# A recurrence with decay and a token mixer on one core: scores in half chunks, and the rest through a copied product of keys and values

## The chip, the cores and the metric

The kernel runs on one core of a Trainium2 chip. The metric is the device time of one execution in microseconds (us). A core has the engines PE (matrix multiply, with PEld its weight load), DVE, ACT and POOL for work on vectors, and SP, which here issues transfers. SBUF is the working memory of 128 partitions, PSUM the memory that PE writes, in eight banks of 512 float32 columns a partition.

## The reference

Four batches, eight heads, 768 tokens, 48 values a head. For each batch and head a 48 by 48 state is carried over the tokens; the mixer behind it works on the eight heads side by side (384 columns).

```python
for t in range(S):
    cur = einsum('bhd,bhe->bhde', u[None] * k[t], v[t])
    y[t] = einsum('bhd,bhde->bhe', r[t], state + cur)
    state = w[t][..., None] * state + einsum('bhd,bhe->bhde', k[t], v[t])
x = y, heads side by side                      # 4 x 768 x 384
W_tok = (x @ w_q) @ (x @ w_k)^T / 8            # taken token by token with x
out = relu(W_tok-mix of x) @ w_out
```

The mixer's two weights are 384 by 64, so its mix is computed as (x w_q) times ((x w_k)^T x), and then relu and w_out.

## The kernel before, in words

The tokens of a batch are cut into three units of 256 tokens, twelve units in all (`unit`, L438). A unit holds two chunks c of 128 tokens. Heads go in pairs: head 2hp in partitions 0 to 63, head 2hp+1 in 64 to 127, 48 of 64 used. With decays as logarithms, the running product inside a chunk becomes a matmul with a triangular matrix, and everything in a chunk can be computed at once.

The steps of a unit, by the names in the code: loads of wg, kg, rg and vg, each 384 KB, on SP (`load`, L301; in batch 3 v comes as `vw` for the whole batch, L306). ACT takes the logarithm lw (L462), POOL casts k and r to bf16 (L472) and v (L581). PE sums the logarithms into PSUM (cw, with CM); ACT takes exp both ways: ep (L500) and en (L505). PE transposes k and r (kr); ks is the copied transpose of k (ACT or DVE), qT = r times k for the bonus (L536), RT = r times ep (L550), KT = k times en (L557 on DVE, L560 mostly on POOL). PE reorders v from two tokens a partition into chunks (vp), and the copy is VB. The bonus is qT times UB (dps), copied as dd, times VB on POOL: Vd (L618).

For each chunk, A is KT by RT: 128 by 128 scores for each of eight heads, 16 matmuls a unit. DVE multiplies them by the mask US into AM (L638, 128x1024 from PSUM, 24 times). KT is also transposed (kb) and scaled into kd, and sn = kd by VB plus the older state gives the next state SB (L696). The result y is yi = RT by the older SB, plus ya = AM by VB (16 matmuls a unit), scaled and added to Vd as X (L754). X is transposed (xt, XT), multiplied by the mixer weights (wk, wq, copied as QK); at the end of a batch T = QK by X (copied as TS), then mx, relu (MX), fp with w_out, os (L393, L399) and the store (L878).

PE has several tile shapes: the full array, two halves by rows (48 or 64 partitions of input), halves by columns, and quarters of 64 by 64. Every matmul has line L250 (`mm`).

The order on each engine is written out: each step has a number in RANK, and ALT says which engine takes a step where there is a choice (D is DVE, A is ACT, P is POOL, E and e are PE, e in parts of the array). `Plan.order` (L86) walks the queues with a duration for each step and gives PSUM banks (one, `bank`, or two, `wide`) and buffers from rings; RINGS has two of most buffers. WARM adds up to 30 multiplies by zeros (Z), where ALT says E.

Of the kernel before, what the change touches and what calls it, by code (L numbers as in the profile page):

```python
# [10 lines left out]
F32 = mybir.dt.float32  # L11
# [22 lines left out]
class Plan:  # L34
# [51 lines left out]
    def order(self):  # L86
# [85 lines left out]
    3, 0, 0, 0, 5, 18, 0, 0, 21, 1, 2, 0, 0, 0, 1, 0, 0, 2, 0, 0, 3, 0, 0, 1, 3, 4, 4, 4, 2, 5,  # L172
    3, 5, 11, 3, 6, 4, 1, 5, 2, 5, 17, 8, 24, 9, 9, 10, 25, 10, 18, 7, 10, 6, 12, 7, 20, 8, 27,
    11, 30, 37, 33, 31, 15, 73, 31, 82, 32, 6, 0, 0, 4, 0, 0, 7, 0, 0, 8, 0, 0, 9, 6, 7, 26, 11,
    12, 23, 28, 10, 13, 12, 14, 8, 34, 14, 36, 15, 15, 40, 17, 45, 21, 41, 18, 48, 20, 53, 23,
    57, 64, 59, 58, 27, 74, 29, 87, 35, 9, 0, 0, 10, 0, 0, 11, 0, 0, 12, 0, 0, 13, 11, 12, 38,
    16, 17, 39, 42, 16, 18, 19, 14, 13, 47, 20, 49, 22, 18, 55, 24, 60, 25, 56, 22, 61, 26, 68,
    69, 72, 70, 30, 80, 36, 88, 36, 94, 38, 97, 40, 109, 49, 47, 0, 0, 102, 42, 120, 53, 50, 0,
    0, 134, 58, 141, 62, 51, 0, 0, 13, 0, 0, 14, 0, 0, 15, 0, 0, 17, 0, 0, 19, 16, 17, 50, 23,
    21, 63, 66, 25, 28, 29, 20, 19, 71, 28, 77, 33, 23, 75, 32, 79, 34, 76, 30, 81, 35, 85, 37,  # L180
    86, 91, 89, 90, 40, 100, 41, 104, 44, 16, 0, 0, 20, 0, 0, 22, 0, 0, 23, 0, 0, 24, 22, 25,
    67, 26, 27, 84, 93, 38, 42, 41, 39, 26, 95, 39, 110, 47, 32, 98, 47, 106, 49, 92, 37, 101,
    46, 105, 48, 115, 119, 118, 117, 54, 128, 59, 139, 60, 19, 0, 0, 21, 0, 0, 24, 0, 0, 25, 0,
    0, 31, 24, 27, 83, 34, 33, 96, 99, 43, 44, 45, 29, 28, 103, 43, 111, 48, 33, 113, 52, 108,
    50, 107, 45, 112, 51, 122, 124, 126, 125, 57, 138, 61, 156, 68, 164, 73, 167, 76, 185, 82,
    54, 0, 0, 176, 78, 211, 97, 52, 0, 0, 183, 81, 213, 99, 53, 0, 0, 26, 0, 0, 28, 0, 0, 27, 0,
    0, 31, 0, 0, 46, 31, 30, 116, 52, 51, 114, 121, 53, 56, 55, 34, 35, 129, 56, 136, 62, 40,
    131, 60, 140, 65, 127, 58, 135, 61, 143, 68, 149, 151, 153, 154, 73, 165, 75, 188, 86, 29,
    0, 0, 30, 0, 0, 33, 0, 0, 32, 0, 0, 50, 36, 38, 123, 55, 54, 132, 137, 57, 64, 63, 39, 37,
    142, 66, 159, 69, 47, 163, 76, 160, 75, 144, 67, 148, 70, 157, 74, 170, 172, 174, 175, 82,  # L190
    187, 83, 199, 91, 35, 0, 0, 37, 0, 0, 34, 0, 0, 38, 0, 0, 59, 41, 42, 145, 65, 64, 146, 150,
    69, 71, 72, 44, 43, 155, 67, 158, 70, 49, 177, 83, 166, 77, 161, 71, 168, 78, 179, 181, 184,
    182, 86, 191, 89, 205, 94, 212, 98, 223, 103, 237, 109, 55, 0, 0, 231, 105, 245, 111, 56, 0,
    0, 234, 109, 248, 113, 57, 0, 0, 36, 0, 0, 41, 0, 0, 40, 0, 0, 45, 0, 0, 46, 0, 0, 63, 46,
    45, 162, 72, 74, 169, 171, 79, 81, 80, 51, 53, 189, 84, 56, 195, 91, 186, 87, 190, 88, 194,
    90, 198, 92, 200, 203, 201, 204, 95, 210, 96, 221, 102, 39, 0, 0, 44, 0, 0, 42, 0, 0, 66,
    50, 48, 173, 77, 79, 178, 180, 80, 85, 84, 52, 54, 192, 87, 59, 207, 98, 197, 93, 193, 88,
    202, 94, 206, 96, 214, 217, 219, 216, 104, 226, 104, 233, 110, 43, 0, 0, 48, 0, 0, 49, 0, 0,
    85, 55, 57, 196, 92, 89, 93, 90, 208, 209, 95, 102, 99, 97, 100, 101, 58, 220, 101, 60, 61,
    215, 103, 224, 106, 218, 100, 222, 105, 225, 229, 227, 230, 228, 232, 107, 235, 106, 238,  # L200
    239, 112, 111, 108, 236, 107, 240, 241, 108, 113, 242, 244, 243, 110, 246, 114, 115, 250,
    253, 118, 116, 59, 0, 0, 61, 0, 0, 247, 112, 116, 251, 252, 114, 119, 58, 0, 0, 60, 0, 0,
    249, 117, 115, 254, 255, 117, 118, 119, 62, 0, 0, 6, 147, 19, 35, 13, 51, 65, 43, 44, 29,
    16, 2, 46, 78, 0, 21, 152, 52, 1, 62, 130, 32, 15, 8, 14, 54, 22, 9, 133, 7,
]
ALT = ("PPDEADAAEDAPPADEAAEAEAAPPDPEADAeDAAAAAAAAPPAPeADEAEAAPPDDEAAeAEDAPPDPeAAAEAAAAAAAAAPPDPE"
       "ADEDEAAPPAPeDAEDEAAPPDPeAAAEDAAAAAADAPPDPAeDEAAPPAPAEAeADPPAAAEADDEAADADDDAADADDAAAEeEEE"
       "eEEEEEeeEeeeEeeeeEeeEeeeE")
# [5 lines left out]
def kernel(  # L214
# [27 lines left out]
    WHOLE = (3,)  # L242
    DIRECT = (0, N - 1)

# [13 lines left out]
    def const(shape, dtype, name):  # L258
# [3 lines left out]
    EW = 132  # L262
# [3 lines left out]

    RINGS = dict(
# [4 lines left out]
        dd=(2, 2 * H, F32), Vd=(2, 2 * DM, BF16), AM0=(2, 1024, BF16), AM1=(2, 1024, BF16),  # L272
# [6 lines left out]
    used = dict.fromkeys(RINGS, 0)  # L279

    uT = const([C, NP * 2], F32, "uT")
    UB = const([C, NP * 2], BF16, "UB")
    wq_f = const([C, NK * DH], F32, "wqf")
    wk_f = const([C, NK * DH], F32, "wkf")
    wo_f = const([C, NK * DM], F32, "wof")
# [152 lines left out]
    def unit(n, batch):  # L438
# [53 lines left out]
        cws = add(("cw", n), {"E": 435}, f_cw, [ln], cw, [lw], mode=1)  # L492

        en, ep = ring("en"), ring("ep")
        ens, eps = {}, {}
        for cs in fine:
            w_ = 512 * len(cs)

# [438 lines left out]
```

## Time and profile before

| what | value |
| --- | --- |
| median of 3 runs | 105.81 us (105.46 to 107.37) |
| the profiled execution's own time | 104.84 us |
| its span, first to last instruction | 103.0 us |
| mean granted PE clock | 0.973 |
| PE, DVE, ACT, POOL busy | 89.3, 81.9, 80.5, 69.5 us |
| matmuls | 1898 |
| moved by DMA | 24.67 MB |
| last load (rg of unit 11) issued | 71.9 us |

A row of the page's fifth part reads: line, engine, operation, out<-in by tile names, sizes of out and in, count; then busy us and mean ns of one; then the idle time of the engine just before, and what ended it. A line of a stretch gives its length, then for PE, PEld, DVE, ACT and POOL the busy us and the count, then the granted clock, the busy share of DMA and GB/s. A line of the timeline gives the start, the length of the run from its first start to its last end, and the count.

### The profile page before, as it was taken

How to read it: one execution, taken by the hardware profiler on the slowest of the kernel's cores; microseconds unless marked ns; L12 is line 12 of the kernel's file. 1: busy time of each engine (PE TensorE's matmuls, PEld its weight loads, DVE VectorE, ACT ScalarE, POOL GpSimd, SP SyncE). 2: the span in 40 equal slices, each digit the busy share in tenths (PEclk: the TensorE clock that was granted, in tenths of full speed). 3: DMA queues.
4: the chain of work that ended last, by engine and by line, in shares of the span. 5: the costliest groups of instructions: out<-in, count | busy, mean ns of one | idle time of the engine just before them, and what ended most of it. 6: DMA issues, size and time to landing. Idle time of an engine off the chain costs nothing.

```text
span 103.0 us, 4462 instructions
## 1 busy us (share of the span) xinstructions
PE 89.3 (87%) x1898; PEld 64.3 (62%) x1898; DVE 81.9 (80%) x140; ACT 80.5 (78%) x121; POOL 69.5 (67%) x81
## 2 busy tenths in 40 slices
PE   5969994999799998999989899879899979999930
PEld 2234753567676966686785787756888648766610
DVE  6628995959989888998999998897999599882800
ACT  6376969769699997999999999888898766766650
POOL 6666393899899976789989997997978504100000
PEclk9999999669999999999999999999999999999995
DMA  1999999999999998999999996999992036204694
GB/s 29 296 325 325 328 259 253 311 296 269 324 255 260 311 293 221 293 282 276 315 314 308 244 293 175 225 166 213 279 376 76 6 153 235 77 0 159 262 353 152
DMA packets 56804, 24.67 MB, mean 240 GB/s; under 512 B 54480, under 2 KB 55632, under 8 KB 56784
## 3 DMA queue, kind: packets, MB, share of 16 engines
q1 hardware_dynamic: 56224, 24.19, 85.0%
q8 instruction: 15, 0.25, 0.9%
q10 hardware_dynamic: 560, 0.20, 0.7%
q14 instruction: 5, 0.04, 0.1%
HBM read 19.66 MB, written 4.72 MB: 237 GB/s over the span
## 4 chain that ended last, share of the span: by engine, by line
PE 51%; DVE 14%; ACT 10%; SPq 9%; DMA 6%; issue 4%; POOL 1%; DVEq 0%; POOLq 0%; ACTq 0%
PE PS L250 51%; SPq L302 9%; DMA kg<-in_k_dram 6%; DVE AM L638 5%; ACT ks L393 3%; DVE X L754 2%; DVE ks L399 2%; ACT ep L500 2%; DVE qT L536 2%; ACT os L393 1%; DVE RT L550 1%; ACT kd L395 1%; ACT en L505 1%; POOL k L472 1%; ACT lw L462 1%
## 5 line engine op out<-in xcount | busy, mean ns | idle before, releaser
L638 DVE TENSOR_TENSOR AM<-PS,US 128x1024 bf16<-128x1024 f32 x24 | 28.9, 1218 | 0.9 <-PE PS L250 0.6
L618 POOL TENSOR_TENSOR Vd<-VB,dd 128x768 bf16<-128x768 bf16 (+1 forms) x14 | 18.0, 1293 | 5.1 <-ACT dd L393 5.1
L560 POOL TENSOR_TENSOR KT<-ks,en 128x1024 bf16<-128x1024 bf16 x8 | 17.0, 2127 | 1.3 <-ACT ks L393 1.3
L500 ACT ACTIVATE ep<-PS 128x1024 bf16<-128x1024 f32 (+1 forms) x14 | 12.6, 918 | 1.7 <-PE PS L250 1.7
L250 PE MATMUL PS<-wo,MX 128*128 128x384 bf16 x72 | 13.4, 326 | 0.7 <-DVE AM L638 0.7
L505 ACT ACTIVATE en<-PS 128x1024 bf16<-128x1024 f32 (+1 forms) x14 | 12.4, 901 | 1.6 <-PE PS L250 1.2
L754 DVE SCALAR_TENSOR_TENSOR X<-PS,gx,Vd 128x768 bf16<-128x768 f32 (+1 forms) x13 | 12.4, 950 | 1.5 <-PE PS L250 1.4
L462 ACT ACTIVATE lw<-wg 128x768 bf16<-128x768 f32 x12 | 10.2, 848 | 4.1 <-DMA wg<-in_w_dram 4.1
L250 PEld LDWEIGHTS <-KT 48*128 48x128 bf16 (+1 forms) x312 | 10.0, 95 | 5.2 <-issue 3.5
L472 POOL CAST k<-kg 128x768 bf16<-128x768 f32 x12 | 9.9, 825 | 4.3 <-DMA kg<-in_k_dram 4.3
L393 ACT COPY os<-PS 128x768 f32<-128x768 f32 (+1 forms) x13 | 9.1, 704 | 3.4 <-PE PS L250 3.2
L472 POOL CAST r<-rg 128x768 bf16<-128x768 f32 x12 | 9.9, 826 | 2.5 <-DMA rg<-in_r_dram 2.4
L250 PE MATMUL PS<-RT,KT 48*128 48x128 bf16 x192 | 9.7, 221 | 0.9 <-DVE qT L536 0.7
L250 PE MATMUL PS<-Z 128*128 128x512 bf16 x23 | 9.2, 502 | 1.2 <-DVE uT L319 1.2
L250 PEld LDWEIGHTS <-MX 128*128 128x128 bf16 x72 | 6.5, 97 | 4.9 <-issue 1.1
L581 POOL CAST v<-vg 128x768 bf16<-128x768 f32 x9 | 7.9, 878 | 2.4 <-DMA vg<-in_v_dram 2.4
L550 DVE TENSOR_TENSOR RT<-PS,ep 128x1024 bf16<-128x1024 bf16 (+1 forms) x14 | 8.3, 607 | 1.0 <-ACT ks L393 0.5
L536 DVE TENSOR_TENSOR qT<-PS,ks 128x1024 bf16<-128x1024 bf16 x12 | 8.2, 682 | 0.9 <-PE PS L250 0.7
L395 ACT ACTIVATE kd<-PS,gk 128x384 bf16<-128x384 bf16 (+1 forms) x10 | 7.0, 712 | 1.7 <-PE PS L250 1.5
L696 DVE TENSOR_TENSOR SB<-PS,ep 128x192 bf16<-128x192 f32 x20 | 7.0, 349 | 1.7 <-PE PS L250 1.5
L250 PE MATMUL PS<-SB,RT 48*128 48x48 bf16 x160 | 7.1, 182 | 1.3
L405 ACT ACTIVATE MX<-PS 128x768 bf16<-128x768 f32 (+1 forms) x10 | 7.5, 753 | 0.7 <-PE PS L250 0.6
(83 smaller groups left out, 188.7 us busy)
## 6 DMA issues: line engine op xcount, KB each, us to landing
wg<-in_w_dram SPq DMA_DIRECT2D x12, 384.0 KB, 5.7
kg<-in_k_dram SPq DMA_DIRECT2D x12, 384.0 KB, 5.9
rg<-in_r_dram SPq DMA_DIRECT2D x12, 384.0 KB, 5.4
vg<-in_v_dram SPq DMA_DIRECT2D x9, 384.0 KB, 5.0
out_dram<-os SPq DMA_DIRECT2D x9, 384.0 KB, 3.1
vw<-in_v_dram SPq DMA_DIRECT2D x4, 288.0 KB, 6.1
out_dram<-os SPq DMA_DIRECT2D x5, 192.0 KB, 2.1
wof<-in_moe_w_out_dram SPq DMA_DIRECT2D x1, 576.0 KB, 5.6
```

The costliest lines, as they stand in the source:

```text
L250: return nc.tensor.matmul(o, l, rr, start=start, stop=stop, skip_group_check=True, is_transpose=trans)
L393: nc.scalar.copy(o, i)
L462: nc.scalar.activation(view(lw.tile, 0, [[64, H], [512, 2], [1, D]]), view(g["wg"].tile, 0, [[D2, H], [D, 2], [1, D]]), ACT.Ln, bias=0.0, ...
L472: op(view(o.tile, 0, [[64, H], [512, 2], [1, D]]), view(g[src].tile, 0, [[D2, H], [D, 2], [1, D]]))
L500: nc.scalar.activation(view(ep.tile, cs[0] * NP * EW + 66, [[EW, NP * len(cs)], [-65, 2], [1, 64]]), at(cw)[:, ds(cs[0] * 512, w_)], ACT.E ...
L505: nc.scalar.activation(en.tile[:, ds(cs[0] * 512, w_)], at(cw)[:, ds(cs[0] * 512, w_)], ACT.Exp, bias=0.0, scale=-1.0)
L536: lambda e: nc.vector.tensor_tensor(view(qT.tile, 0, [[512, 2], [1, 512]]), turned(512), view(ks.tile, 0, [[512, 2], [1, 512]]), ALU.mult),
L550: nc.vector.tensor_tensor(o, x, y, ALU.mult)
L560: x.tensor_tensor(o, view(ks.tile, cs[0] * 512, dims), y, ALU.mult)
L618: nc.gpsimd.tensor_tensor(Vd.tile[:, cols], VB.tile[:, cols], view(dd.tile, cs[0] * H, [[1, len(cs) * H], [0, D]]), ALU.mult)
L638: AMs[c] = add(("AM", n, c), {"D": 1221}, lambda e, c=c, A=A: nc.vector.tensor_tensor(view(AM[c].tile, 0, [[C, 8], [1, C]]), view(at(A), 0 ...
L754: nc.vector.scalar_tensor_tensor(view(X.tile, (2 * i + c0) * DM, [[DM, nc_], [1, DM]]), view(at(y), 0, [[512, nc_], [1, DM]]), gx, view(Vd ...
```

## The change

Scores are computed only within half chunks of 64 tokens. A is now a matmul of 64 by 64 for each head, chunk and half, on quarters of the array; the two halves of a chunk stand in the two halves of the partitions, so that one AM of 128x1024 holds a whole unit, where there were two (in the first and the last unit, two of 128x512). What the second half takes from the first goes through a product: kv = kd by VB over the first 64 tokens, 16 matmuls a unit, copied to the new tile KV (ACT or DVE) and scaled back. ya is now AM by VB on quarters, in two turns with a drain between, with KV by RT for the second half after each turn: 48 matmuls a unit instead of 16.

For this the tokens inside a chunk are ordered by halves of 64, and inside those even and odd tokens in 32s; masks, permutations and views follow. ep has a column more for each half (EW 136 instead of 132, steps of 34 and 68), which a new step sh copies, on POOL in nine units and on DVE in three; RT waits for sh. In units 0 and 1 (FULL) the transposes of k and r use the whole array: 8 matmuls of 128 columns instead of 16 on halves. vp always uses halves. In the last unit of a batch kb and kd are made for both chunks. `load_whole` issues four transfers where there were two. The bonus u is loaded in rows of heads (UR), cast, transposed by one multiply and copied as UB. RANK and ALT are new, and with them which engine takes which copy.

```diff
+        dd=(2, 2 * H, F32), Vd=(2, 2 * DM, BF16), AM=(2, 1024, BF16), KV=(2, NCHP * D, BF16),
...
+            def f_sh(e, cs=cs):
+                n4 = NP * len(cs)
+                op = nc.vector if e == "D" else nc.gpsimd
+                op.tensor_copy(view(ep.tile, cs[0] * NP * EW + 68, [[EW, n4], [1, 1]]),
+                               view(ep.tile, cs[0] * NP * EW + 32, [[EW, n4], [1, 1]]))
...
+                        if full:
+                            mm(view(o, place + hp * pair + j * 32,
+                                    [[NP * pair, 2], [64, 2], [1, 32]]), x, ID16, trans=True)
...
-                        mm(x[:, ds(hh * 512 + hp * C, C)],
-                           KT.tile[ds(hh * 64, D), ds((c * NP + hp) * C, C)],
-                           RT.tile[ds(hh * 64, D), ds((c * NP + hp) * C, C)])
+                        for q in range(2):
+                            cols = ds((c * NP + hp) * C + q * 64, 64)
+                            mm(x[ds(q * 64, 64), ds(hh * 512 + (c * NP + hp) * 64, 64)],
+                               KT.tile[ds(hh * 64, D), cols], RT.tile[ds(hh * 64, D), cols])
...
+        for cs in fine:
+            def f_AM(e, cs=cs):
+                dims = [[512, 2], [64, NP * len(cs)], [1, 64]]
+                nc.vector.tensor_tensor(
+                    view(AM.tile, cs[0] * NP * 64, dims), view(at(A), cs[0] * NP * 64, dims),
+                    view(US, 0, [[0, 2], [0, NP * len(cs)], [1, 64]]), ALU.mult)
...
+            def f_kv(e, cs=cs):
+                x = at(kv)
+                for c in cs:
+                    for h in range(H):
+                        hp, hh = divmod(h, 2)
+                        mm(x[ds(hh * 64, 64), ds((c * NP + hp) * D, D)],
+                           kd.tile[ds(0, 64), ds(64 + (c * H + h) * 128, 64)],
+                           VB.tile[ds(0, 64), ds(c * DM + h * D, D)])
...
+            def f_KV(e, cs=cs):
+                w_ = ds(cs[0] * NP * D, NP * D * len(cs))
+                copy(e, KV.tile[:, w_], at(kv)[:, w_], 1 / UNIT)
...
+        def local(turn, cs, begun):
+            for hp in range(NP):
+                for h in (2 * hp, 2 * hp + 1):
+                    for c in cs:
+                        q = c ^ turn
+                        o = of(c, h)[ds(q * 64, 64), :]
+                        mm(o, AM.tile[ds(q * 64, 64),
+                                      ds((h % 2) * 512 + (c * NP + hp) * 64, 64)],
+                           VB.tile[ds(q * 64, 64), ds(c * DM + h * D, D)],
+                           start=(not begun[c] and h == 0), stop=False)
+            for hp in range(NP):
+                for c in cs:
+                    hh = c ^ turn
+                    o = of(c, 2 * hp + hh)[ds(64, 64), :]
+                    mm(o, RT.tile[ds(hh * 64, D), ds((c * NP + hp) * C + 64, 64)],
+                       KV.tile[ds(hh * 64, D), ds((c * NP + hp) * D, D)], start=False, stop=True)
...
-                for h in range(H):
-                    hp, hh = divmod(h, 2)
-                    mm(of(c, h), AM[c].tile[:, ds(hh * 512 + hp * C, C)],
-                       VB.tile[:, ds(c * DM + h * D, D)],
-                       start=(not yis[c] and h == 0), stop=True)
+                begun = {c: bool(yis[c]) for c in cs}
+                local(1, cs, begun)
+                nc.tensor.drain()
+                local(0, cs, begun)
```

## The prediction

> **What bounds the kernel now.** I read the page's first two parts, then the chain that ended last, then the busy times by 8 us stretches, and last the timeline of one stretch, where the pitch of the matrix multiplies can be worked out.
>
> ```profile
> PE 89.3 (87%) x1898; PEld 64.3 (62%) x1898; DVE 81.9 (80%) x140; ACT 80.5 (78%) x121; POOL 69.5 (67%) x81
> PE   5969994999799998999989899879899979999930
> ...
> PE 51%; DVE 14%; ACT 10%; SPq 9%; DMA 6%; issue 4%; POOL 1%; DVEq 0%; POOLq 0%; ACTq 0%
> ...
> L638 DVE TENSOR_TENSOR AM<-PS,US 128x1024 bf16<-128x1024 f32 x24 | 28.9, 1218 | 0.9 <-PE PS L250 0.6
> ```
>
> PE is the fullest engine, and half of the chain is PE. DVE's largest group is AM, which the change halves. But DVE waits seldom and is waited for seldom: in the list of waits, PE waits for AM 1.2 us in all. The stretches show how even the load is:
>
> ```profile
> 32.00:40.00 8.00, 7.34 (x204) 5.65 (x199) 6.81 (x12) 7.34 (x11) 6.39 (x8) 1.00 1.07 286
> 40.00:48.00 8.00, 7.52 (x175) 5.80 (x173) 7.87 (x11) 7.16 (x12) 7.03 (x7) 1.00 1.01 265
> 48.00:56.00 8.00, 7.50 (x177) 5.60 (x175) 7.45 (x12) 7.57 (x10) 7.66 (x7) 1.00 1.15 312
> 88.00:96.00 8.00, 7.81 (x86) 5.63 (x85) 5.26 (x11) 5.34 (x10) 0.00 (x0) 1.00 0.21 80
> ```
>
> The columns are PE, PE's weight load, DVE, ACT, POOL, granted clock, DMA share and GB/s. Up to 78 us the four engines are all at about 90%, so none can be relieved alone; behind 84 us the chain is almost only PE (9.3 us in one piece from 88.5). A busy PE is not a PE at its peak, so I take pitches from the timeline: a run's busy time less one instruction's mean, over the count less one.
>
> ```profile
> 45.05 0.40 PE L250 MATMUL PS<-RT,KT 48*128 48x128 bf16 x8
> ...
> 45.52 0.41 PE L250 MATMUL PS<-ID,k 64*128 64x64 bf16 x16
> ...
> 46.42 0.57 PE L250 MATMUL PS<-VB,AM 128*128 128x48 bf16 x16
> ```
>
> RT,KT: (0.40 - 0.22)/7 = 26 ns. ID,k: (0.41 - 0.19)/15 = 15 ns. VB,AM: (0.57 - 0.18)/15 = 26 ns. In the same way ID,KT 48x48, two row halves in turn, is 12 ns; SB,RT in runs of 4, all on one row half, is 29 ns; X-by-identity 128x128 is 57 ns. Between runs of different tile shape about 100 ns pass. Adding these up for every run (with 216 ns for each zero filler) gives 68 us of multiplying and 11 us of shape changes, of the 93 us between the first real multiply (5.2 us) and the last (98.8 us). The rest, some 14 us, PE truly waits, 6 of it before 20 us, when loads are still arriving (k waits for its load 1.3 us at 16.7). From 20 us on PE is nine tenths full.
>
> **The change, part by part.** Instruction counts are those of the two built programs.
>
> *Scores (A).* 192 multiplies of 128 columns become 384 of 64 columns on four quarters of the array. Before: 192 x 26 ns = 5.0 us. After: no row shows four quarters in a steady run; the nearest, ID,k (64 columns, two tiles), is 15 ns, and twice as many tiles would halve it to 7. I take 10: 3.8 us, **-1.2** (from -2.3 to +0.8).
>
> *Masked scores times values (ya).* 192 full multiplies (5.0 us) become 384 of AM by VB and 192 of the copied product KV by RT, both on two quarters at a time. Bounds: 12 ns (ID,KT, two tiles) and 29 ns (SB,RT, one tile). I take 15, as ID,k is the nearest in rows: 576 x 15 = 8.6, **+3.6** (+1.9 to +11.7). Each of 13 steps now holds a drain, at about the 100 ns of a shape change: **+1.3** (0 to 2). In the last unit each half runs alone on one quarter: 48 x (29 - 15) = **+0.7**.
>
> *The product kv.* 192 new multiplies on two quarters, same bounds, 15 ns taken: **+2.9** (2.3 to 5.6).
>
> *Transposes.* In units 0 and 1 64 of them become 32 over the full array: 32 x 57 - 64 x 15 = **+0.9**, while PE waits for loads there anyway. The other regrouped transposes, the value permutation (16 quarter multiplies become 16 half ones) and two more fillers come to **-0.2**. Shape changes are 105 before and 104 after: nothing.
>
> PE in all: -1.2 + 3.6 + 1.3 + 0.7 + 2.9 + 0.9 - 0.2 = **+8.0 us**, from +3 to +21 with all ends together.
>
> *DVE.* AM: 24 x 1.218 = 28.9 becomes 10 x 1.218 plus 4 of half size (0.61 by X 128x384 from PSUM, to 0.75): 14.8, **-14.1**. The new step order hands DVE other work: 6 copies XT (0.55), 3 to 4 kd (0.62), 2 KT (0.97), 2 KV (0.55, as the QK copy of 384), and one or two each of os, MX, ks, QK and a cast, together about +12. Net **-2**. *ACT* gets 8 KV of 384 columns and 4 of 192 (0.58 as kd 128x384, 0.35: 6.0) and loses 6 XT, 2 os, kd, MX and others: net **-2**. *POOL* loses two KT and two casts and gains ten copies of one column (0.19, as the UB cast): net **-4**. RT now reads ep in steps of 34 values instead of 66; I take nothing, since its rows stay bf16; the other end is the rate of AM, 1.22 us for RT's 0.69, twelve times: +6 on DVE.
>
> *Queues.* SP issues eight loads vw instead of four (1.1 to 2.2 us each before); they are for the last batch, needed at 73 us and issued from 63, so nothing if the pace holds, up to +2 if they push wg, rg and kg of unit 11 behind them. The bonus path at the start (rows, one multiply, one copy) lies beside the first loads: nothing, up to +0.3. The copied column (sh) puts POOL's queue between ep and RT; its place is ahead of KT, mostly. I take nothing and price it as a rival. The other new wait is ya's for KV: behind kd (ACT or DVE), kv (PE) and one copy of 0.58, while ya's old input AM is ready half a step sooner. Behind ya on PE stands whatever is planned next, mostly wk and wq of an earlier unit; a late KV would hold those too. KV needs no more than AM did (A, then 1.22 on DVE), so I take nothing here, up to 0.3 a unit.
>
> ***The sum.*** Of PE's +8.0, the work of units 0 and 1 and of most of unit 2 lies where PE waits for loads: 0.9 of the transposes and about 2.3/12 of the other 7.1, together 2.3. There remain +5.7 on a PE that is nine tenths full. What can take it up: PE waits about 8 us after 20 us, for DVE, ACT and POOL, which lose 8 us in all. I let PE's waits shrink by as much as half of that, 3.7 us, because three engines lose little each and all stay at 85 to 90% of the middle. Net **+2.0 us**. The profiled execution took 104.84 us (span 103.0 and 1.8 around it), so 106.8 for such a one; the median of the three runs is 105.81, 1.0 above it, so **107.8 us** for a median.
>
> **Rivals.** *Slow weights on narrow tiles (0.17).* If a tile of 64 columns takes its weights slowly, ya and kv go at the 29 ns of one tile: 576 x 14 + 192 x 14 = 10.8 us more on PE, of which about 8.5 lie after 20 us with no cover left; some wait is absorbed, so +4 to +8 on the forecast: 112 to 116. For it: weight loads of QK 128x64 average 108 ns against 97 of full ones. Against: X by QK on these tiles runs at 70 ns for 384 columns, two tiles at full speed, though a long multiply hides its weights. [...]
>
> *DVE's relief is worth more (0.22).* Then the AM steps were what staggered PE: in the chain AM holds 5% (5.5 us), and PE's waits after 20 us fall from 8 to 2 us, with quarters at their low ends (PE +4, 3 after 20 us): -3 net, 102.8, range 101 to 104.5. Against: list of waits, 1.2 us of PE for AM.
>
> *POOL's hop stalls RT (0.13).* POOL takes 2.13 us for KT and 1.48 for Vd; if the column copy stands behind one of them in half of its nine units and RT, qT, A slip 1 us each time, +4 to +5 on the forecast: 111 to 112.5. It decides once RT is later than A's turn on PE, since PE works in order. Against: POOL gives up 4 us.
>
> *Nothing shows (inside the forecast).* If kv, ya and the rest only fill PE's gaps, the time stays at 105.8.
>
> **Numbers.** Forecast 0.48, own range 105.5 to 110; rivals 0.17, 0.22 and 0.13. The range that leaves out 2 in 10 runs from the middle of the DVE case to the lower edge of the slow weights: 102.8 to 112.5. Faster by over 2% means below 103.7: most of the DVE case and nothing else, 0.17. Within 2% (to 107.9, about what a measurement of this kernel can tell): a bit over half of the forecast and the rest of the DVE case, 0.32. Slower: 0.51, split over the forecast's upper half and two rivals; the likeliest single time still lies just inside the bound.
>
> **What would show it.** Right: AM at about 15 us of DVE; PE runs of 16 AM by VB of about 0.4 us, KV by RT of 8 about 0.3, kv of 16 about 0.4; DVE and ACT still near 80; PE with fewer waits from 20 to 80 us, and the last load landing at 78 us or later. Slow weights: those runs twice as long. POOL's hop: RT idle before it, released by POOL. DVE's relief: PE's chain share above 60% and a last load before 75 us. Wrong altogether: if the narrow runs take under 10 ns each, or if RT or ep take longer than 0.69 and 1.04 us.

## The result

The changed kernel takes **125.94 us** (median of four executions, 122.88 to 129.39) beside 106.03 us for the kernel before in the same rounds: a ratio of **1.164** (95% interval 1.152 to 1.176), taken from the two executions in which PE's granted clock was highest (0.909 and 0.958), since the four differ by 6.5 us and the slower ones have less clock (0.875 and 0.858). The forecast was 107.8, and the range ended at 112.5.

The page of the kernel after, in the order of the lines shown of before (the instruction queue's line added):

```profile
PE 110.1 (86%) x2695; PEld 80.5 (63%) x2695; DVE 82.7 (65%) x152; ACT 79.1 (62%) x123; POOL 66.7 (52%) x93
...
PE   6999998696759998798998939999998998999970
...
PEclk9999999999995599958999985555999999657998
...
q8 instruction: 21, 0.34, 1.0%
...
PE 68%; issue 12%; POOL 11%; ACT 3%; DVE 3%; POOLq 0%; DVEq 0%; ACTq 0%
...
L681 DVE TENSOR_TENSOR AM<-PS,US 128x1024 bf16<-128x1024 f32 (+1 forms) x14 | 15.0, 1068 | 4.7 <-PE PS L255 3.5
```

AM has its 15.0 us, as worked out, and DVE, ACT and POOL are busy about as long as before, in a span of 127.7 us instead of 103.0. What is new stands in three lines. PE's slices have dips to 3, 5 and 6 in mid-kernel. The granted clock, which was at half for 3.41 us before (18.91 to 22.32 us), is at half for 30.7 us in all: for 6.83, 3.41, 13.65 and 6.83 us from 37.80, 54.87, 75.35 and 109.48 us (counted from 7 us on, where its records begin; 3.41 us is the shortest of these spells, and the others are two or four times as long). And the chain has 12% "issue": time in which nothing that the profile shows was waited for. The rows of the clock and of the instruction queue before:

```profile
PEclk9999999669999999999999999999999999999995
...
q8 instruction: 15, 0.25, 0.9%
```

The same by stretches (columns as in the lines shown of before: PE, weight load, DVE, ACT, POOL, granted clock, DMA share, GB/s):

```profile
32.00:40.00 8.00, 5.71 (x187) 4.62 (x185) 4.18 (x8) 5.64 (x8) 4.16 (x6) 0.86 0.95 241
48.00:56.00 8.00, 6.51 (x207) 4.98 (x208) 6.55 (x10) 5.49 (x9) 8.00 (x9) 0.93 1.10 297
75.00:83.00 8.00, 7.34 (x189) 5.69 (x189) 3.36 (x5) 4.46 (x6) 2.82 (x5) 0.52 0.48 151
88.00:96.00 8.00, 7.80 (x285) 6.23 (x288) 5.70 (x10) 5.80 (x12) 6.23 (x5) 0.94 0.14 53
```

While the loads run, PE gets through about as many multiplies in 8 us as before (175 to 204 there), although the kernel now has 2,695 of them instead of 1,898. Once the loads are over (88 to 96 us, DMA at 0.14) it does 285, at nearly full clock. So multiplies seem to go faster where nothing is being loaded, though the mix differs from stretch to stretch. The other three engines have gaps nearly everywhere (POOL is full from 48 to 56 us): in the list of waits it is mostly PE that they wait for.

Where PE stands still, the timeline shows no reason (start, length, engine, line, operation and count; in brackets the idle time before the run and what ended it):

```profile
34.22 0.18 PE L255 MATMUL PS<-UB,qT 128*128 128x2 bf16 x1
36.49 0.31 PE L255 MATMUL PS<-UB,qT 128*128 128x2 bf16 x7 [2.09 <-issue]
```

These lines are one run of eight multiplies with the same inputs: the first is issued, then PE stands for 2.09 us, then the other seven follow. No engine and no load can be late for the second multiply that was not late for the first. In the list of waits these stops add up (waited for: us in all, times, longest):

```profile
PEld L255 <- issue: 26.4, 75, 2.9
...
PE PS L255 <- issue: 7.2, 7, 2.1
```

Before, the list had no such line for PE itself of 0.2 us or more. Counting PE's instructions (each multiply is two, a weight load and a multiply: 2,695 of each) gives the pattern: all seven stops come at instruction 180 or so of a block of 256 (index modulo 256 between 167 and 188 in all kernels here), though not every block has one. And the instruction queue, q8, moved 21 packets of 16 KB (16,384 bytes, 0.88 to 1.37 us each) where before there were 15. PE has 5,390 instructions, before 3,796, which is 257 and 253 to a packet: blocks of 256, and so, worked out, 64 bytes an instruction. At all seven stops PE goes on 1.3 to 1.6 us after the end of a packet.

### The profile page after: what moved, and what is told of

Its sections match the earlier page's. It is cut to its first block, busy times and chain, and to the rows that moved or that the text cites. A ratio compares the mean times of both kernels' runs of the same rounds, so it can differ in the third digit from the quotient of the medians.

```text
span 127.7 us, 6099 instructions
## 1 busy us (share of the span) xinstructions
PE 110.1 (86%) x2695; PEld 80.5 (63%) x2695; DVE 82.7 (65%) x152; ACT 79.1 (62%) x123; POOL 66.7 (52%) x93
## 4 chain that ended last, share of the span: by engine, by line
PE 68%; issue 12%; POOL 11%; ACT 3%; DVE 3%; POOLq 0%; DVEq 0%; ACTq 0%
PE PS L255 68%; POOL KT L595 5%; POOL Vd L660 2%; POOL k L490 1%; POOL r L490 1%; POOL v L616 1%; DVE KT L595 1%; ACT ep L518 1%; ACT lw L480 1%; DVE ks L410 1%; ACT VB L404 1%; DVE AM L681 1%; ACT os L404 0%; ACT kd L406 0%; DVE KT L592 0%
## 5 line engine op out<-in xcount | busy, mean ns | idle before, releaser
L595 POOL TENSOR_TENSOR KT<-ks,en 128x1024 bf16<-128x1024 bf16 x6 | 12.8, 2130 | 11.4 <-PE PS L255 6.2
L681 DVE TENSOR_TENSOR AM<-PS,US 128x1024 bf16<-128x1024 f32 (+1 forms) x14 | 15.0, 1068 | 4.7 <-PE PS L255 3.5
L843 DVE SCALAR_TENSOR_TENSOR X<-PS,gx,Vd 128x768 bf16<-128x768 f32 (+1 forms) x13 | 12.3, 953 | 7.8 <-PE PS L255 7.8
L255 PEld LDWEIGHTS <-RT 48*64 48x64 bf16 (+1 forms) x352 | 12.6, 106 | 4.3 <-issue 3.9
L255 PEld LDWEIGHTS <-KT 48*64 48x64 bf16 (+2 forms) x544 | 9.5, 110 | 8.2 <-issue 5.5
L255 PEld LDWEIGHTS <-kd 64*64 64x64 bf16 (+1 forms) x352 | 11.8, 110 | 2.9 <-issue 2.0
L255 PE MATMUL PS<-VB,AM 64*64 64x48 bf16 x384 | 12.5, 196 | 1.3
L255 PE MATMUL PS<-VB,kd 64*64 64x48 bf16 (+1 forms) x352 | 13.3, 193 | 0.1
L255 PEld LDWEIGHTS <-AM 64*64 64x64 bf16 x384 | 9.7, 116 | 3.7 <-issue 3.0
L480 ACT ACTIVATE lw<-wg 128x768 bf16<-128x768 f32 x12 | 10.1, 843 | 1.7 <-DMA wg<-in_w_dram 1.7
L255 PE MATMUL PS<-KV,RT 48*64 48x48 bf16 x192 | 10.5, 197 | 0.0
L255 PE MATMUL PS<-CM,lw 64*128 64x128 bf16 x192 | 9.0, 239 | 1.1 <-issue 1.1
```

The lines of the kernel that those rows point to most:

```text
L255: return nc.tensor.matmul(o, l, rr, start=start, stop=stop, skip_group_check=True, is_transpose=trans)
L480: nc.scalar.activation(view(lw.tile, 0, [[64, H], [512, 2], [1, D]]), view(g["wg"].tile, 0, [[D2, H], [D, 2], [1, D]]), ACT.Ln, bias=0.0, ...
L595: x.tensor_tensor(o, view(ks.tile, cs[0] * 512, dims), y, ALU.mult)
L681: nc.vector.tensor_tensor(view(AM.tile, cs[0] * NP * 64, dims), view(at(A), cs[0] * NP * 64, dims), view(US, 0, [[0, 2], [0, NP * len(cs)] ...
L843: nc.vector.scalar_tensor_tensor(view(X.tile, (2 * i + c0) * DM, [[DM, nc_], [1, DM]]), view(at(y), 0, [[512, nc_], [1, DM]]), gx, view(Vd ...
```

## First theory: instructions come late

**Theory.** PE's instructions arrive in blocks of 256, and beside loads a block takes longer than PE needs for it. In the trace of after, blocks that PE had to wait for followed each other in 4.4 to 6.7 us while loads ran; the kernel before used one in 4.7 to 7.4 us and so hardly waited; the changed kernel would use one in 3.1 to 5 (an estimate, from its blocks at full clock in that trace less the stops). **Rival.** PE's added work alone makes the time, and the stops are something else.

### The kernel before with more instructions, and both kernels without loads

*The kernel before, split.* The same products, cut into more multiplies by columns (2,705 instead of 1,898), nothing else changed. The cut of A as an example; cw, wq, mx and fp are cut the same way:

```diff
-                    for hh in range(2):
-                        mm(x[:, ds(hh * 512 + hp * C, C)],
-                           KT.tile[ds(hh * 64, D), ds((c * NP + hp) * C, C)],
-                           RT.tile[ds(hh * 64, D), ds((c * NP + hp) * C, C)])
+                    for q in range(2):
+                        for hh in range(2):
+                            mm(x[:, ds(hh * 512 + hp * C + q * 64, 64)],
+                               KT.tile[ds(hh * 64, D), ds((c * NP + hp) * C, C)],
+                               RT.tile[ds(hh * 64, D), ds((c * NP + hp) * C + q * 64, 64)])
```

> The kernel before with the same array work in shorter pieces: A and the sums of logarithms in two pieces of 64 columns instead of one of 128, the output product in four of 96 instead of one of 384, wq and mx in pieces of 64. Nothing is left out. PE gets some 2,705 matmuls instead of 1,898, as many as the changed kernel (2,695), with none of its narrow tiles, its product KV, its hop over POOL or its order. Theory I (PE runs out of instructions: they come in blocks over the same DMA engines as the loads, PE uses a block up before the next is there, and the clock falls after each stop): stops of 0.5 us and more in the middle of runs, mean granted clock below 0.95, 112 to 124 us. Theory W (the narrow work itself, its longer chain and the new order): only the pieces' own cost, about 2 us of PE, so 107 to 110 us and no stops.

Measured: **112.04 us** (111.37 to 112.70), ratio 1.053 (1.044 to 1.063). In its list of waits:

```profile
PE PS L250 <- issue: 4.6, 8, 1.1
```

A kernel that had no stops has them once its multiplies are cut, six of them between 38 and 76 us, each at index 182 or so in 256, of 0.3 to 1.1 us. That the clock would fall behind them was wrong: it stayed at 0.96 to 0.98.

*Without loads.* The loads of w, k, r and v of units 4 to 11 are left out (the v of batch 3 stays), so the arithmetic goes on with old data and the output is not the reference's.

```diff
-                                     lambda e, ap=ap, x=g[name].tile: load(b, i, x, ap),
+                                     (lambda e, ap=ap, x=g[name].tile: load(b, i, x, ap)) if n < 4 else None,
```

The kernel before without these loads:

> The kernel before with the same loads left out, as the measure of what the cut alone brings (waits for loads fall away). Both theories: a little faster than before, 98 to 104 us; theory I adds that the distance from the changed kernel without loads is only PE's added work, 4 to 9 us, where it was 17 to 20 us with loads.

Measured: 106.25 us (104.35 to 107.72); ratio 0.987 (0.973 to 1.000). Loads cost the kernel before next to nothing, and the 98 to 104 us expected was too low.

The split kernel without them:

> The kernel before in shorter pieces, with the loads of units 4 to 11 left out as well. Theory I: without traffic the blocks come in time, so it lies within 3 us of the kernel before without these loads. If the pieces themselves cost time on PE (a rival for whatever the split kernel shows), it stays as far above as the split kernel with loads is above the kernel before.

Measured: 109.35 us (106.70 to 110.16), with one stop of 0.45 us left of the six: 2.7 us less than with the loads. It is 3.1 us above the kernel before without these loads, just outside the 3 us expected, so the shorter pieces themselves cost something too.

The changed kernel without them:

> The changed kernel, with the loads of w, k, r and v left out for units 4 to 11, which work on the older contents of the same four buffers; every instruction of PE, DVE, ACT and POOL stays. From about 25 us on there is little traffic beside the instructions. Theory I: no stops in the middle of runs after 25 us, granted clock 0.95 or more, 104 to 112 us. Theory W: the narrow work and its chain remain, so it gains no more than the kernel before gains by the same cut, and stays at 117 us or above.

Measured: **119.85 us** (115.24 to 120.61). About 6 us go with the loads, and PE's stops shrink to 2.4 us in the list of waits; but the theory expected 104 to 112, and this is a miss: the time lies where the rival had it (117 or above), though the gain is more than the rival allowed, and the kernel before without loads is 13.6 us away instead of 4 to 9. Two falls of the clock remain, at 34 and 99 us, the second with only 0.45 us of idle PE in the window ahead of it. So blocks of instructions are a part of the time, not all, and the clock needs a cause of its own.

### The supply by itself

A kernel with PE and loads alone: 1,280 multiplies on four quarters in turn, 64 columns each (2,560 instructions, ten blocks), then 768 on two row halves, first with nothing loading, then beside all 48 loads. It multiplies zeros and its output is zeros.

```python
def quarter(x, y, bank, rows=64, cols=64, w_=512):
    mm(PS[ds(y * 64, cols), ds(bank * 512, w_)], Z[ds(x * 64, rows), ds(0, cols)],
       Z[ds(x * 64, rows), ds(0, w_)])
def narrow(n_):
    for x in range(n_ // 4):
        for q in range(4):
            quarter(q // 2, q % 2, 1 + q, rows=48, w_=64)
```

> Only TensorE and loads: 1,280 multiplies of 48x64 tiles and 64 columns on four quarters in turn (2,560 instructions, 10 blocks of 256), then 768 of 48x128 on two row halves (6 blocks), first with no load under way, then the same again while all 48 unit loads run. The output is zeros. Theory 'supply' (instructions come in blocks of 256, and a block takes about 1 to 2 us with no loads and 4.4 to 6.5 us beside them): the narrow stretch takes 11 to 20 us without loads and 40 to 65 us beside them, the wider one 20 us without and 25 to 39 us beside. Theory 'work' (instructions are always there): 8.2 x 1,280 = 10.5 us and 26 x 768 = 20 us, both times.

The timeline of the narrow stretch, first with nothing loading:

```profile
54.31 1.92 PE L54 MATMUL PS<-Z 48*64 48x64 bf16 x128 [1.92 <-issue]
57.76 1.92 PE L54 MATMUL PS<-Z 48*64 48x64 bf16 x128 [1.53 <-issue]
61.49 1.92 PE L54 MATMUL PS<-Z 48*64 48x64 bf16 x128 [1.81 <-issue]
```

and then beside the loads:

```profile
136.09 1.92 PE L54 MATMUL PS<-Z 48*64 48x64 bf16 x128 [4.27 <-issue]
140.92 1.92 PE L54 MATMUL PS<-Z 48*64 48x64 bf16 x128 [2.90 <-issue]
144.92 1.92 PE L54 MATMUL PS<-Z 48*64 48x64 bf16 x128 [2.08 <-issue]
```

Each run is 128 multiplies, one block, and ahead of each is a stop. From run to run it is 3.45 us (at times 3.73) with nothing loading, and 3.7 to 5.1 us beside the loads, 4.55 on average over eight blocks. The stretches:

```profile
47.00:81.00 34.00, 18.54 (x1283) 17.02 (x1283) 0.00 (x0) 0.00 (x0) 0.00 (x0) 0.57 0.02 5
95.00:115.00 20.00, 12.28 (x769) 11.56 (x768) 0.00 (x0) 0.00 (x0) 0.00 (x0) 1.00 0.02 4
130.00:175.00 45.00, 19.36 (x1285) 17.52 (x1284) 0.00 (x0) 0.00 (x0) 0.00 (x0) 0.54 1.01 267
```

The narrow stretch takes 33 us (47.4 to 80.1) without loads and 44 us beside them, where the multiplies alone would need 10.5 at full clock. The clock was at half for most of it (0.57 and 0.54), but at half clock a block of multiplies still takes only 1.92 us, or 19 us for all ten. Work alone is refuted. My figure for no loads (11 to 20 us) was too low as well: even then a block takes 3.45 us. The first block or so of each stretch runs through at 8.2 ns a multiply, so that much seems to lie ready; then PE stands ahead of each block, for 1.5 to 2.1 us without loads and 1.8 to 4.3 beside them. The trace of the transfers fits a wait for each block's own packet: in these stretches the packet of 16,384 bytes takes 0.9 to 1.9 us, and PE goes on 1.1 to 1.5 us after its end. The wider stretch took 19.9 us without loads, as both theories expected, but not by the work: PE was busy for 12.3 us of it, since its multiplies of 64 columns ran at 15 ns and not at the 26 that I had taken. It stood 1.3 to 1.7 us ahead of each block here too, at full clock:

```profile
103.45 2.04 PE L54 MATMUL PS<-Z 48*128 48x64 bf16 x128 [1.69 <-issue]
```

Beside the loads it took 21.6 us, under the 25 to 39 expected, but the loads ended early in it (DMA at 0.02 from 197 us on) and the clock fell, so it says little.

The kernel before, which used a block in 4.7 us or more, hardly stood at the edges of its blocks. Here, where the multiplies of a block take 1.92 us, PE stands at each edge, and a block comes every 3.45 us without loads and every 4.55 us on average beside them.

## Second theory: the clock counts rows

**Theory.** The granted clock falls where too little of the array has worked in a window of 3.41 us, however busy PE looks. The spells of the clock in the traces of before and after last 3.41 us or multiples of it, and that is taken as the window. In the traces the time that PE is busy does not tell the windows ahead of a fall from the others (in the trace of after, the window from 27.56 us has PE idle for 1.10 us and kept the clock, the one from 106.07 us has 0.36 us of idle and lost it), but the share of the array at work does. I first counted cells (rows times columns of the tile, by the columns streamed). **Rival.** Only gaps in PE's work count.

### The clock by itself

PE alone, with nothing to wait for and no loads: 17 us each of multiplies of 512 columns on a part of the array, with 14 us of the full array between (`quarter` as above).

```python
full(160)
for _ in range(80): quarter(0, 0, 1)                                   # one quarter, 64x64
full(64)
for _ in range(80): quarter(0, 0, 1); quarter(1, 1, 2)                 # two quarters at once
full(64)
for _ in range(80): quarter(0, 0, 3, rows=64, cols=128)
full(64)
for _ in range(80): mm(PS[ds(0, 48), ds(4 * 512, 512)], Z[:, ds(0, 48)], Z)   # 128x48
full(64)
for _ in range(80): quarter(0, 0, 5, rows=48, cols=128)
```

and then, in the same way, one full multiply to five quarter ones, and 128 x 32.

> Only TensorE works here (zeros, 512 columns in every multiply, nothing to wait for, no loads): stretches of 17 us on a part of the array, with 14 us of the full array between them. The parts, as a share of the array's cells: one quarter 64x64 (0.25), two quarters at once (0.5), 64 rows x 128 columns (0.5), 128x48 (0.375), 48x128 (0.375), one full multiply to five quarter ones (0.375), 128x32 (0.25). The output is zeros. Theory 'share' (the clock falls to half when the cells at work in a window of 3.41 us, weighted by time, come to under about a third of the array, however busy TensorE is): half clock in the two stretches of 0.25, full clock in the two of 0.5, those of 0.375 at the edge, either way. Theory 'idle' (only gaps in TensorE's work bring the clock down, as I took it in the prediction): no fall in any stretch, 216 ns a multiply throughout.

The seven stretches, in that order, each without its edges:

```profile
41.00:54.00 13.00, 13.00 (x62) 6.44 (x61) 0.00 (x0) 0.00 (x0) 0.00 (x0) 1.00 0.00 1
72.00:85.00 13.00, 13.00 (x124) 6.67 (x122) 0.00 (x0) 0.00 (x0) 0.00 (x0) 1.00 0.00 0
103.00:116.00 13.00, 13.00 (x62) 5.64 (x60) 0.00 (x0) 0.00 (x0) 0.00 (x0) 1.00 0.01 1
135.00:148.00 13.00, 13.00 (x62) 6.22 (x61) 0.00 (x0) 0.00 (x0) 0.00 (x0) 1.00 0.01 1
172.00:190.00 18.00, 18.00 (x44) 6.30 (x43) 0.00 (x0) 0.00 (x0) 0.00 (x0) 0.50 0.00 0
211.00:230.00 19.00, 18.75 (x76) 6.93 (x75) 0.00 (x0) 0.00 (x0) 0.00 (x0) 1.00 0.00 0
249.00:262.00 13.00, 13.00 (x62) 5.82 (x60) 0.00 (x0) 0.00 (x0) 0.00 (x0) 1.00 0.00 0
```

PE is busy all the time in them (18.75 of 19 us in the sixth), and the granted clock (third value from the right) is 0.50 in exactly one: 48 rows by 128 columns. So gaps are not needed, and the rival is out. But cells are out as well: a quarter of 64 x 64 and a strip of 128 x 32 have a quarter of the cells and keep the clock, while 48 x 128 has three eighths and loses it. What that stretch has least of is **rows**: 48 of 128.

### Which rows

The same kernel with other shapes: 56 x 128, 52 x 128, 48 x 128 on two row halves in turn, 64 x 32, 48 x 128 followed at once by 64 x 128, and 40 x 128.

> TensorE alone again (zeros, 512 columns a multiply, no waits, no loads), now on other numbers of rows, 17 us each with 14 us of the full array between: 56 x 128, 52 x 128, 48 x 128 on two row halves in turn, 64 x 32, then 48 x 128 followed at once by 64 x 128, then 40 x 128. The output is zeros. Theory 'rows' (the clock falls where the rows at work, weighted by time, come to 3/8 of the array or less in a window; columns do not count): 56 and 52 rows, the two halves in turn and 64 x 32 keep the full clock, 48 and 40 rows alone lose it within two windows of 3.41 us; whether 64 rows bring it back is open, and tells where the clock rises again. Theory 'cells' (rows times columns count): 64 x 32 (an eighth of the cells) loses it as well. Theory 'form' (it was a matter of 48 rows not filling a tile of 64): 56, 52 and 40 rows lose it too.

```profile
41.00:54.00 13.00, 13.00 (x62) 5.69 (x61) 0.00 (x0) 0.00 (x0) 0.00 (x0) 1.00 0.01 1
73.00:86.00 13.00, 13.00 (x62) 5.67 (x61) 0.00 (x0) 0.00 (x0) 0.00 (x0) 1.00 0.01 1
104.00:117.00 13.00, 13.00 (x124) 5.88 (x122) 0.00 (x0) 0.00 (x0) 0.00 (x0) 1.00 0.01 1
135.00:148.00 13.00, 13.00 (x62) 5.58 (x60) 0.00 (x0) 0.00 (x0) 0.00 (x0) 1.00 0.01 1
172.00:190.00 18.00, 18.00 (x44) 6.30 (x43) 0.00 (x0) 0.00 (x0) 0.00 (x0) 0.50 0.00 0
193.00:203.00 10.00, 10.00 (x25) 3.40 (x23) 0.00 (x0) 0.00 (x0) 0.00 (x0) 0.50 0.00 0
240.00:261.00 21.00, 21.00 (x51) 7.28 (x50) 0.00 (x0) 0.00 (x0) 0.00 (x0) 0.50 0.00 1
```

"Rows" holds in all of them: 56, 52 and two times 48 rows keep the clock, 48 and 40 alone lose it, and 64 x 32 keeps it with an eighth of the cells. The sixth line settles what was open: 64 rows, which keep a full clock, do not bring a halved one back, though the full array does (the clock kernel is at 0.50 from 172 to 190 us and, after a stretch of the full array, at 1.00 from 211 us). Both follow from one count. At half clock only half as many columns pass in a window (51 multiplies touch the 21 us of the last line, 62 touch the 13 us of the first: 429 and 217 ns each, less two cut at the edges), so 64 rows come to 0.25 of a full array at full clock, and the full array to 0.5. Falling has its edge between 48 rows (0.375, lost) and 52 (0.406, kept), rising between 0.25 and 0.5, so both can have the same one, at about 3/8; that it is the same is an estimate.

That count can be taken in the kernels' own traces: for each window of 3.41 us (the grid is given by the steps of the clock, above), the sum over its multiplies of columns times rows/128, divided by 8,192 columns, 16 multiplies of 512 (at 216 ns each a window holds 15.8 of them). Windows ahead of a fall, without those in which the kernel ends:

| kernel | share of rows in the windows ahead of a fall |
| --- | --- |
| before | 0.37 |
| split | 0.30 |
| after (two traces) | 0.24, 0.35, 0.27, 0.36; 0.37, 0.31, 0.26 |
| after without loads | 0.39, 0.34 |

All other windows of these kernels at full clock are above 0.38, and those at half clock from which it rose are at 0.38 or more. It isn't exact: some multiplies are missing from a trace, two windows at half clock with 0.44 and 0.55 did not raise it, and two windows near the end of kernels told of below kept it at 0.33. Before, the windows hold 0.64 on average. By that average a stop of 1.4 us takes a window to 3/8, and a shorter one does where the window has fewer rows; so does the last unit of the changed kernel, where AM by VB and KV by RT go on one quarter at a time, every 33 to 53 ns for 48 columns of 64 rows or fewer: 24 / 33 ns over 8,192 / 3,413 ns is 0.30, and less at 53 ns. That explains the fall at 109.5 us, behind a window with 0.36 us of idle. In the kernel with 48 rows the clock fell with no idle at all.

### The same in the kernel

*Four fillers at the end.* Multiplies of zeros over the full array, two ahead of each chunk's first part of the output in the last unit: more work for PE, but more rows.

```diff
+                if end and first:
+                    for _ in range(2):
+                        mm(at(ys[cs[0]]), Z[:, ds(0, C)], Z)
```

> The changed kernel with four more multiplies of zeros over the full array (216 ns each, 0.86 us of work added) in the last unit, two ahead of each chunk's first part of the output, where the array works on single quarters. Theory 'share': the window there was at 0.29 of the array and the clock fell behind it for 6.8 us, with 0.36 us of idle in it; four fillers bring it to 0.4 or more, the fall at the end goes, the six multiplies wo,MX behind it take 0.98 us in place of 1.92, and the kernel is 1 to 3 us faster than the changed one beside the same kernel before (ratio 1.13 to 1.16 against 1.164). Theory 'idle or chance': the fall stays, and the added work makes it 0.9 us slower (1.17).

Measured: 124.12 us (123.76 to 126.07), beside 105.69 for the kernel before: ratio 1.191 (1.185 to 1.198), where 1.13 to 1.16 was expected. The fall at the end is gone from its trace, but it is absent from the second trace of the changed kernel as well (told of below), which has no fillers. The clock of this kernel, and of that second trace:

```profile
PEclk9999999999999999998699999655579999999997
```

```profile
PEclk9999999999995589997569999555557999999999
```

So the missing fall does not show by itself that the fillers took it away. What speaks for them is the count. The window at the end with fillers in it, which stayed at full clock, has a share of 0.33 in the trace; one filler's multiply is missing there (two weight loads of Z at 105.41 and 105.52 us, one multiply), and with it the share is 0.39. Without the three fillers in it, at 512 columns each, it would be 0.20, an estimate. In time nothing can be claimed: the median is 1.8 us lower than the changed kernel's, the ratio, from other executions, is higher, and the executions differ by more than that.

*Fillers, and no loads.* The changed kernel without loads, with those four fillers and two each in units 1, 2 and 3 ahead of the scores: 2.2 us of work added.

> The changed kernel without the loads of units 4 to 11 (its output is not the reference's), with two fillers of 216 ns in units 1, 2 and 3 ahead of the scores and four in the last unit: 2.2 us of work added to the run without loads, which took 115.2 to 120.6 (clock 0.92 to 0.96) with falls at 34 and 99 us. Theory 'share': those falls go, mean clock 0.97 or more, 112 to 115 us, though work was added; what is then left over the unchanged kernel without loads (106.25) is TensorE's added work, 6 to 8 us. Theory 'idle or chance': the falls stay, and it takes 117 to 123 us.

Measured: **114.80 us** (114.29 to 117.79) against 119.85 without the fillers. PE's clock over the 40 slices of the span, without and with the fillers:

```profile
PEclk9999999999975559999999999999999998559996
```

```profile
PEclk9999999999999999999999999999999999999995
```

The clock stays up: its mean is 0.971 to 1.000 in the four executions, where it was 0.920 to 0.962 without the fillers, and the two windows that had lost it at 0.39 and 0.34 have counterparts at 0.41 and 0.42 that keep it. With 2.2 us of work added, the kernel is 5 us faster by the medians; between the fastest executions (114.29 and 115.24) it is 1 us. What is left by the medians, 114.8 - 2.2 = 112.6 against 106.25 for the unchanged kernel without loads, is **6.4 us**: PE's added multiplies, and 1.7 us of stops that its list of waits still has.

## Fewer instructions, more rows

If that is the cause, the changed kernel should gain from anything that takes away instructions or keeps rows at work, even if it adds multiplying. Three kernels beside each other on one chip: the changed kernel again; the same with the transposes of r and k over the full array in every unit; and the same without the product of keys and values.

> The changed kernel as it is, beside the two kernels below on one chip: 122 to 129 us, with stops of TensorE near one index in 256 of its instructions and falls of its clock behind them. Both theories expect the same of it; it is what the other two are compared with.

Measured: 124.84 us (118.64 to 130.82; clocks 0.956 down to 0.861), beside 105.93 for the kernel before.

```diff
-    FULL = (0, 1)
+    FULL = tuple(range(N))
```

> The changed kernel with the transposes of r and k over the full array in all units, not in units 0 and 1 alone: 160 multiplies and so 320 of TensorE's instructions fewer (19.8 blocks of 256 in place of 21), more rows of the array at work, but 10 x (16 x 57 - 32 x 15) = 4.3 us more of multiplying. Theory 'supply and clock' (blocks of instructions that come late, and a clock that falls where few rows work): the stops and falls shrink by about as much as the work grows, 121 to 126 us, at most level with the changed kernel. Theory 'work' (TensorE's added work makes the time): 3 to 4.5 us slower than the changed kernel, 128 to 130.

Measured: **119.86 us** (115.73 to 123.95; clocks 1.000 down to 0.919). Its lines of PE, clock and instruction queue:

```profile
PE 108.4 (89%) x2535; PEld 80.9 (66%) x2535; DVE 82.0 (67%) x152; ACT 79.1 (65%) x123; POOL 66.9 (55%) x93
...
PEclk9999999999996579995999999995999999869995
...
q8 instruction: 20, 0.33, 1.1%
```

160 multiplies are gone, 4.3 us of multiplying by their pitches are added, and the kernel does not become 4 us slower but 5 us faster by the medians (both ranges are wide and overlap), and 2.9 between the fastest executions. That is below the 121 to 126 expected. Where its clock stayed full throughout, it took 115.73.

```diff
-                    for h in range(H):
-                        hp, hh = divmod(h, 2)
-                        mm(x[ds(hh * 64, 64), ds((c * NP + hp) * D, D)],
-                           kd.tile[ds(0, 64), ds(64 + (c * H + h) * 128, 64)],
-                           VB.tile[ds(0, 64), ds(c * DM + h * D, D)])
+                w_ = NP * D * len(cs)
+                mm(x[:, ds(cs[0] * NP * D, w_)], Z[:, ds(0, C)], Z[:, ds(0, w_)])
...
-                    mm(o, RT.tile[ds(hh * 64, D), ds((c * NP + hp) * C + 64, 64)],
-                       KV.tile[ds(hh * 64, D), ds((c * NP + hp) * D, D)], start=False, stop=True)
```

> The changed kernel without the product of keys and values: the 192 multiplies kv become 14 of zeros, and the 192 of the copied product by r are left out, so the half chunks lack what the first half gives to the second; the output is not the reference's. Everything else, copies and waits too, stays. 740 of TensorE's instructions fall away (18.2 blocks in place of 21), and by their pitches about 5 us of multiplying. Theory 'supply and clock': 113 to 118 us, a mean clock of 0.95 or more, three blocks' worth of stops gone. Theory 'work': 5 us, 119 to 122.

Measured: **115.90 us** (113.39 to 117.33), ratio 1.080 (1.066 to 1.094); clocks 0.969 to 0.918, a little lower than expected in three of four. 370 multiplies less, worth 5 us by their pitches, save 9 us by the medians against the changed kernel beside it (124.84), where work alone would have left 119 to 122. But between the fastest executions (113.39 and 118.64) they save 5.3 us, about what the work alone gives, so this kernel does not decide between the theories.

None of these variants comes near the kernel before, which stays the fastest of all that ran with loads and the whole computation.

## Why the prediction was wrong

**Where the time came from.** In the profiled execution the span grew by 24.7 us. The clock was at half for 30.7 us instead of 3.4, which at most doubles the time of the work in it (six multiplies wo,MX take 1.92 us at half clock, from 113.78 us, and 0.97 at full, from 117.54): 27.3 / 2 = 13.7 us. PE stood for instructions for 7.2 us. That leaves at least 3.8 for the rest, where the forecast had +2.0. The clock's part can be checked between two executions of the same kernel: the span times the missing clock is 127.7 x 0.125 = 16.0 us in the profiled one (129.39 us) and 116.9 x 0.044 = 5.1 us in the fastest of the second set (118.64). The difference is 10.8 us, and so is that of the times. Not every pair fits as well: 122.88 us was measured with the same 5.1 us of missing clock. A straight line through all eight executions of the changed kernel rises by 0.73 us for each us of missing clock and comes to 116 us at full clock. By it, as an estimate, the clock makes 0.73 x (16.0 - 2.8) = 10 us of the profiled execution's 24.7 (2.8 is the missing clock before), and work and stops together some 15. So the two causes are shown, but the split between them is rough. The runs without loads and without falls give it from the other side: 6.4 us of work and small stops (1.7 of stops, so 4.7 of work, which the sum had let shrink to 2.0), and then 12 to 13 us that come with loads and falls (112.6 to 124.84 and 125.94).

**The step that failed** is in the sum: that PE's added multiplies cost their pitch and nothing else. The prediction had some 800 more multiplies and priced none of them as instructions that have to arrive, although the page had 15 packets on q8. Nor was the clock anywhere in the sum: the one window of half clock at 19 us was not mentioned, and that gaps or narrow work of PE would bring the clock down again was not asked (the expectation of the clock kernel says that I took gaps to do so in the prediction; the prediction has nothing on it). PE's waits for DVE, ACT and POOL did fall, from about 7.5 us to 3.1 by the lists of waits (3.7 were let go), though a slower PE waits less in any case, and the 7.2 us for instructions came in their place.

**The terms one by one** (pitches from runs at full clock in the trace of after):

- *Scores (A)*: 8.2 to 8.4 ns a multiply where 10 was taken. Right in kind, a little better.
- *ya and KV*: AM by VB 16.3 ns, KV by RT about 20 where runs of both follow each other, 15 taken for both: 384 x 16.3 + 192 x 20 = 10.1 us instead of 8.6. *kv* 15.7 to 16.4 instead of 15. Nearly right; 1.7 us too low together.
- *Last unit on one quarter*: 33 to 53 ns instead of 29, and, not priced at all, too few rows for the clock.
- *DVE, ACT, POOL*: AM 15.0 (14.8 worked out); RT unchanged at 610 ns, so ep's steps of 34 cost nothing; ACT -1.4 (-2), POOL -2.8 (-4), DVE +0.8 instead of -2. Right that no great relief was left there, and without weight for the result.
- *Queues, sh, the wait for KV*: nothing, as taken. RT waits for nothing of POOL in the list of waits, and PE for no copy KV.

**The rivals.** *Slow weights* forecast the nearest time (112 to 116), by a mechanism that isn't there: it needed 29 ns for ya and kv, and they take 16 (KV by RT about 20). Short multiplies on tiles of 64 columns had no visible price here: two quarters in turn ran at 16 ns, four at 8.2. *DVE's relief* named PE's share of the chain above 60% as its sign, and it is 68%, but because PE became slower. *POOL's hop* shows in no wait of RT. That the kernel could end outside all of them was given no chance beyond the two in ten left over.

**The signs.** Those for the forecast mostly came true: AM at 15 us, DVE and ACT near 80, fewer waits of PE for other engines. The time was lost where no sign had been named, in "issue" and in the clock's row.

**What stays open.** Why PE goes on only 1.1 us or more after a block has landed (1.1 to 1.5 in the kernel of PE and loads, 1.3 to 1.6 in the trace of after), and what in the loads delays a block (their number of packets, their bytes or their queue) was not taken apart. The edge of the clock near 3/8 of the rows is shown for single shapes (48 rows lose it, 52 keep it); the count over mixed windows is an approximation that misses in a few.

## What to carry to other kernels

Cutting a product into more and smaller multiplies has a price that no pitch shows: count PE's instructions, two a multiply, divide by the 256 of a block here, and compare with the time of the stretch. A block came every 4.55 us on average beside loads and every 3.45 without, and where PE used them faster it stood, in the changed kernel for 7.2 us in all. Look at how many of the array's 128 rows are at work, not at how many columns or at how busy PE is: in the traces of before and after, windows of 3.41 us with 0.24 to 0.37 of the rows at work were followed by half clock for 3.41 to 13.65 us, and 3.41 us of it take up to 1.7 us of work, so a stop of 1 to 2 us can cost its length again and more. Where a line of a trace says "issue" in the middle of a run of like multiplies, look first at the instruction queue and not for an engine or a load.

## What the runs showed that was not expected

- PE's instructions come in blocks of 256: 3.45 us from block to block with no loads, 4.55 on average beside them, with stops of 1.5 to 2.1 us and 1.8 to 4.3 us, where PE used a block in 1.9 us at half clock (1.05 at full clock, by 8.2 ns a multiply).
- The clock weighs rows: 52 of 128 keep it, 48 lose it, at 100% busy; 64 x 32, an eighth of the array's cells, keeps it. At half clock 64 rows do not bring it back, the full array does.
- Multiplies of zeros made a kernel faster: ten of them, 2.2 us, took 5 us off the changed kernel without loads by the medians, and 1 us between the fastest executions.
- Four quarters in turn take 8.2 ns a multiply of 64 columns, and at 48 rows that lasts for a block or so until the instructions run out.
